# Attention and a gated MLP on one core: plain fp32 products with v in the first four head pairs, new planner durations, and a weight decode that works through PSUM

## The chip, the cores and the metric

The kernel runs on one core of a Trainium2 chip. Its time is the device time of one execution in microseconds (us). The profile shows five engines of the core: PE (TensorE: matrix products and transposes), DVE (VectorE), ACT (ScalarE), POOL (GpSimd) and SP (SyncE, which here only issues DMAs). Each engine runs its own list of instructions strictly in order and waits on semaphores for the others.

## What is computed

Attention with rotary embedding over 8 batches of 8 heads (sequence 576, head dimension 64), and then, on each batch, a gated MLP whose gate is mixed along the sequence.

```python
q_rot, k_rot = (rotate(q), rotate(k))
scores = scale * np.matmul(q_rot, k_rot.transpose(0, 1, 3, 2))
scores = scores - np.max(scores, axis=-1, keepdims=True)
attn = np.exp(scores)
attn = attn / (np.sum(attn, axis=-1, keepdims=True) + 1e-09)
return np.matmul(attn, v).astype(np.float32)
...
h = np.maximum(x @ w_in, 0.0)
u, v = (h[..., :d_ff // 2], h[..., d_ff // 2:])
...
v_n = (v - mu) / np.sqrt(var + 1e-06)
v_s = np.einsum('ts,bsd->btd', w_spatial, v_n) + b_spatial[None, :, None]
gated = u * v_s
return (gated @ w_out).astype(np.float32)
```

The inputs are float32, but the weights w_in and w_out come as 64-bit floats, so the kernel has to turn two 32-bit words into one float32 itself.

## The kernel before

**Precision.** Most products run on fp32r, a reduced float32 format of PE. To keep float32 accuracy an operand is split: ACT rounds it (`round_hi`, L298), a second engine subtracts the rounded part from the original (`rest_lo`, L301), and a product is made of three fp32r products: high by high, high by low, low by high.

**Attention.** The 64 heads are taken as 32 pairs, four to a batch. For each pair `prepare` loads q and k into two buffers `st` (stage), applies the rotation (L384 multiplies by a table half, L388 adds the two halves), splits them, copies rows into the stationary layouts `qs`, `ks`, `qz` by DMA, makes the low part of k (`lk`), and splits v into `vs` (ACT L298, POOL L423). `scores` makes nine score tiles of 128 x 576 for a pair (L459); DVE takes the row maximum (`nmx`, L467) and ACT the exponential with its row sum (`e`, L469). `values` works in three chunks of three tiles: PE turns the exponentials around 128 keys at a time (`tp`, L487), ACT takes the high part out of PSUM (`eh`, L498), DVE the low part (`el`, L301), and PE multiplies with v into `pv` (L511). In the first five pairs (`SUMMED = 5`) the three products of a step go one after the other into the same 64 rows of `pv`, and ACT copies them out (L525); in the later pairs high and low part of v are one operand 128 wide, ACT copies half of `pv` to `avt` (L535) and DVE adds the halves (L533). `normalise` sends the row sums through DRAM to spread them over partitions (`rt`, `rb`), multiplies (L565) and splits the result `x` for the MLP.

**MLP.** Four pairs make a batch; its MLP has four products: `pa` (W_in's second half, L599), `pb` (W_in's first half, L622), `pc` (along the sequence, L640) and `pd` (W_out, L655), with the normalisation on DVE and ACT between them.

**Weight decode.** `decode` handles 12 pieces of 128 x 512. Its five DVE steps (L328 twice, L334, L336, L337) shift, mask and combine the words, ACT does two (L333, and the high part), and the low part goes to POOL or DVE. All operands lie in SBUF. The steps of DVE are marked as holding the port that DVE and POOL share (`port=True`).

**Order.** Nothing is issued in the order written. Each step is entered in `Program` with a key, a duration per engine and the buffers it needs; `run` simulates the engines and, whenever one is free, issues the ready step with the lowest key, so the durations in the table and the numbers of buffers (`SLOTS`) decide what order the engines' lists have. A step with two costs (`pair_op`) goes to whichever engine takes it first. PSUM has two buffers for scores (`sc`), one for `pv` and three called `pm` for transposes and MLP products.

Of the kernel before, what the change touches and what calls it, by code (L numbers as in the profile page):

```python
# [211 lines left out]
def tile_attention_gated_mlp(  # L212
# [93 lines left out]
    def decode(key, where, at, src):  # L306
# [19 lines left out]

        def bits(out, w, s1, s2, op0, op1=None):
            return lambda: ts(out=out(), in0=word(w), scalar1=s1, scalar2=s2, op0=op0, **({"op1": op1} if op1 else {}))  # L328
# [5 lines left out]
        op(DVE, 600, key, lambda: stt(out=sg.tile, in0=word(1), scalar=-(2**31), in1=sg.tile, op0=ALU.bitwise_and, op1=ALU.bitwise_or), r=[t1], w=[sg], port=True)  # L334
        op(DVE, 335, key, bits(lambda: word(1), 1, 0xFFFFF, 0x100000, ALU.bitwise_and, ALU.bitwise_or), w=[t1], port=True)
        op(DVE, 602, key, lambda: stt(out=word(1, F32), in0=word(0, U32), scalar=2.0**-32, in1=word(1), op0=ALU.mult, op1=ALU.add), r=[t0], w=[t1], port=True)  # L336
        scaled = lambda: stt(out=sg.tile.bitcast(F32), in0=word(1, F32), scalar=2.0**-20, in1=sg.tile.bitcast(F32), op0=ALU.mult, op1=ALU.mult)  # L337
# [106 lines left out]
    def scores(i, a, t, lk, sm, key, e, n_e):
# [24 lines left out]
        op(ACT, 717, key + K_EXP, lambda: nc.scalar.activation(e[:, e0:e0 + S].rearrange("p (c n) -> p c n", c=2), tops(), AF.Exp, bias=nmx.tile, scale=1.0, accum_out=sm[:, at:at + 1]), r=[pt, nmx, *([(e, 0)] if n_e == 1 else [])], w=[(e, n_e), ("sums", i % 2, at)], new=[] if n_e == 1 else [e])  # L469
# [322 lines left out]
```

## Time and profile before

| | |
|---|---|
| time, median of 3 runs | 1005.13 us (1003.97 to 1006.08) |
| the profiled execution: its own time | 1004.86 us |
| the profiled execution: span of the trace | 1003.1 us |
| busy PE / DVE / ACT / POOL | 944.0 / 698.1 / 757.2 / 596.0 us |
| PE's granted clock, mean | 0.995 |
| DMA packets, bytes, mean rate | 56694, 126.19 MB, 126 GB/s |

The span runs from the first to the last instruction; the execution's own time is 1.8 us longer. A line of the profile names the kernel's line, the engine, the operation, and output <- input by the program's names; a row of the timeline starts with the start and the duration in us, and ends with the idle time ahead of it and what ended it. PE rows are pipelined: a product's duration includes its way through the array, so the distance between the starts of two rows is what a product costs in a stream.

### The profile page before, as it was taken

The page shows a single profiled execution, that of the slowest core. Times are in us where ns is not written, and L with a number is a line of the kernel's source. Part 1 is how long each engine was busy: PE and PEld are TensorE (multiplying, and loading weights), DVE is VectorE, ACT ScalarE, POOL GpSimd, SP SyncE. Part 2 cuts the span into 40 slices and gives each one's busy share as a digit, 9 for nine tenths or more (in the row PEclk, how much of TensorE's full clock was granted, in tenths as well). Part 3 has the DMA queues.
Part 4 walks back from the last instruction along what each step waited for, and adds up shares of the span by engine and source line. Part 5 has one row for each costly group of instructions (what it writes and reads, how often), then busy time and mean ns, then how long its engine had stood idle before and what let it go on. Part 6 is the DMA issues. An engine that isn't in the chain of part 4 may idle for free.

```text
span 1003.1 us, 19763 instructions
## 1 busy us (share of the span) xinstructions
PE 944.0 (94%) x6692; PEld 874.5 (87%) x6692; DVE 698.1 (70%) x1557; ACT 757.2 (75%) x1850; POOL 596.0 (59%) x512
## 2 busy tenths in 40 slices
PE   3868888999999999999999999999999999999998
PEld 2657767999889998999989998899989998899898
DVE  6888989886776758676676767766576766767340
ACT  4877788777887778777787778877797777977452
POOL 3665666566566757566576756657675765773121
PEclk9999999999999999999999999999999999999999
DMA  8786443445453454445533464443544355431101
GB/s 276 219 226 198 134 135 77 119 106 157 130 134 94 116 152 122 122 116 158 147 88 104 122 170 125 126 128 88 153 119 131 104 159 145 104 88 32 60 1 48
DMA packets 56694, 126.19 MB, mean 126 GB/s; under 512 B 13329, under 2 KB 13329, under 8 KB 56594
## 3 DMA queue, kind: packets, MB, share of 16 engines
q1 hardware_dynamic: 56594, 124.94, 45.6%
q8 instruction: 53, 0.87, 0.4%
q14 instruction: 47, 0.39, 0.1%
HBM read 66.03 MB, written 9.58 MB: 75 GB/s over the span
## 4 chain that ended last, share of the span: by engine, by line
PE 57%; ACT 18%; DVE 11%; DMA 8%; issue 4%; SPq 2%; POOL 0%; ACTq 0%; DVEq 0%; POOLq 0%
PE pc L640 10%; PE tp L487 9%; PE sc L459 9%; PE pd L655 9%; PE pv L511 9%; PE pb L622 7%; ACT e L469 5%; ACT eh L498 5%; PE pa L599 4%; DMA st<-in_qk_dram 3%; DVE nmx L467 2%; SPq L295 2%; DMA qs<-st 2%; DVE el L301 2%; ACT vv L682 2%
## 5 line engine op out<-in xcount | busy, mean ns | idle before, releaser
L498 ACT ACTIVATE eh<-tp 128x384 fp32r<-128x384 f32 (+1 forms) x576 | 246.7, 432 | 73.7 <-PE tp L487 69.7
L301 DVE TENSOR_TENSOR el<-tp,eh 128x384 fp32r<-128x384 f32 x384 | 210.6, 551 | 87.4 <-ACT eh L498 83.7
L469 ACT ACTIVATE e<-sc,nmx 128x576 f32<-128x576 f32 x288 | 213.4, 741 | 46.7 <-DVE nmx L467 43.3
L467 DVE TENSOR_REDUCE nmx<-sc 128x1 f32<-128x576 f32 x288 | 215.4, 750 | 44.0 <-PE sc L459 41.5
L487 PE MATMUL tp<-ident,e 128*128 128x128 f32 x1344 | 227.3, 276 | 16.1 <-DVE el L301 9.5
L487 PEld LDWEIGHTS tp<-ident,e 128*128 128x128 f32 x1344 | 165.9, 139 | 39.1 <-issue 10.8
L511 PE MATMUL pv<-eh,vs 128*128 128x384 f32 (+3 forms) x740 | 193.6, 319 | 2.6 <-ACT x L525 1.9
L384 POOL TENSOR_TENSOR st<-st,tabq 128x576 f32<-128x576 f32 x57 | 82.0, 1449 | 147.6 <-DMA st<-in_qk_dram 136.7
L459 PE MATMUL sc<-ks,qs 128*128 128x288 f32 x640 | 139.1, 308 | 24.4 <-DMA ks<-st 16.9
L622 PE MATMUL pb<-x,wi 128*128 128x288 f32 x768 | 144.1, 308 | 7.8 <-DVE eh L301 4.5
L640 PE MATMUL pc<-wsp,vn 128*128 128x288 f32 x768 | 143.8, 304 | 1.7 <-DVE eh L301 1.7
L655 PE MATMUL pd<-g,wo 128*128 128x288 f32 x768 | 142.3, 304 | 1.0 <-DVE el L301 0.4
L459 PEld LDWEIGHTS sc<-ks,qs 128*128 128x128 f32 x640 | 105.6, 193 | 35.0 <-issue 16.4
L511 PE MATMUL pv<-el,vs 128*64 128x192 f32 (+1 forms) x512 | 130.6, 296 | 2.0 <-DVE el L301 2.0
L599 PE MATMUL pa<-wi,x 128*128 128x512 f32 x448 | 131.0, 405 | 0.0
L622 PEld LDWEIGHTS pb<-x,wi 128*128 128x128 f32 x768 | 113.7, 190 | 14.6 <-PE pb L622 5.3
L459 PE MATMUL sc<-lk,qz 128*128 128x288 f32 x576 | 124.8, 299 | 0.0
L511 PEld LDWEIGHTS pv<-eh,vs 128*128 128x128 f32 (+1 forms) x740 | 116.5, 175 | 9.3 <-ACT x L525 2.9
L640 PEld LDWEIGHTS pc<-wsp,vn 128*128 128x128 f32 x768 | 114.7, 189 | 5.1 <-PE sc L459 2.9
L655 PEld LDWEIGHTS pd<-g,wo 128*128 128x128 f32 x768 | 113.8, 189 | 5.1 <-ACT ob L658 1.6
L301 DVE TENSOR_TENSOR eh<-tp,eh 64x256 fp32r<-64x256 f32 x192 | 68.3, 356 | 70.9 <-ACT eh L498 59.6
L459 PEld LDWEIGHTS sc<-lk,qz 128*128 128x128 f32 x576 | 93.9, 191 | 0.0
(139 smaller groups left out, 1372.8 us busy)
## 6 DMA issues: line engine op xcount, KB each, us to landing
st<-in_qk_dram SPq DMA_DIRECT2D x64, 576.0 KB
ks<-st SPq DMA_DIRECT2D x128, 160.0 KB
qs<-st SPq DMA_DIRECT2D x128, 144.0 KB
vr<-in_v_dram SPq DMA_DIRECT2D x32, 320.0 KB
qz<-st SPq DMA_DIRECT2D x64, 144.0 KB
out_dram<-ob SPq DMA_DIRECT2D x32, 288.0 KB
ws<-in_w_spT_dram SPq DMA_DIRECT2D x2, 576.0 KB
tabs<-in_tab_dram SPq DMA_DIRECT2D x1, 576.0 KB
```

The source lines that it names most:

```text
L301: eng.tensor_tensor(out=lo, in0=src, in1=hi.bitcast(F32), op=ALU.subtract)
L384: f = lambda e: e.tensor_tensor(out=st[j][:, cols], in0=st[j][:, cols], in1=(tabs if j else tabq)[:, cols], op=ALU.mult)
L459: nc.tensor.matmul(pt[:, c * 512:c * 512 + HALF], lhsT=lhsT, rhs=rhs[:, k0 + c * HALF:k0 + (c + 1) * HALF], start=(n == 0), stop=(n == len ...
L467: op(DVE, 665, key + K_MAX, lambda: nc.vector.tensor_reduce(out=nmx.tile, in_=tops(), op=ALU.max, axis=AX.XY, negate=True), r=[pt], w=[nmx ...
L469: op(ACT, 717, key + K_EXP, lambda: nc.scalar.activation(e[:, e0:e0 + S].rearrange("p (c n) -> p c n", c=2), tops(), AF.Exp, bias=nmx.tile ...
L487: nc.tensor.transpose(out=tp[:e.shape[1], m * P:m * P + P], in_=e, identity=ident)
L498: nc.scalar.activation(h, p, AF.Copy)
L511: nc.tensor.matmul(pv[0:rows, c1:c2], lhsT=vs[:, kt, h, vp, :], rhs=part[:, c1:c2], start=(kt == 0 and n == 0 and c1 == 0), stop=last)
L599: nc.tensor.matmul(pm.tile, lhsT=lhsT, rhs=win[1, d][:, j, :], start=(d == 0 and n == 0), stop=(d == 3 and n == len(todo) - 1))
L622: nc.tensor.matmul(pm[:, :HALF], lhsT=win[0, d][:, i, f * P:(f + 1) * P], rhs=x[d][:, at:at + HALF], start=(d == 0 and n == 0), stop=(d == ...
L640: nc.tensor.matmul(pm[:, :HALF], lhsT=lhsT, rhs=rhs, start=(t == 0 and n == 0), stop=(t == 4 and n == 1))
L655: nc.tensor.matmul(pm[:, :HALF], lhsT=wout[d,][:, i, m * P:(m + 1) * P], rhs=gs[d][:, at:at + HALF], start=(d == 0 and n == 0), stop=(d == ...
```

## The change

Three things change together.

The first four pairs (`PLAIN = 4`) get a routine of their own, `attention_plain`. They are no longer split: `e` is turned around as before, but each transposed block is copied out of PSUM once (`et`, by ACT or DVE, whichever the planner finds free) and multiplied as plain fp32 with the v that was loaded (`vr`). The two heads of a pair go to rows 0 to 63 and 64 to 127 of `pv`. The tiles are grouped differently: a first chunk of six tiles (three of each head) and a second of three, where tile 4, which holds the tails of both heads, needs a small copy on POOL (`e1`). The splitting of v and the adds are gone there. All later pairs, pair 4 now included, use the 128-wide form.

The decode keeps its intermediate in one of the three `pm` buffers of PSUM instead of SBUF, so that each DVE step has at most one operand in SBUF and no longer claims the shared port; the low part always goes to DVE.

The table is changed: durations of many small steps, POOL's cost, the decode's keys, and `SLOTS` (among others `vs` from 2 to 1, `vraw` from 1 to 2, `e2` from 3 to 5, `e1` from 4 to 2, `eh` from 8 to 7). In `normalise` the add of 1e-9 to the row sums moves from DVE to ACT.

```diff
 SLOTS = {
-    "stage": 2, "lk": 1, "vraw": 1, "vs": 2, "e2": 3, "e1": 4, "eh": 8, "rb": 1, "x32": 1, "avt": 1, "xg": 7, "m": 4,
-    "small": 4, "nmx": 3, "rt": 2, "sc": 2, "pv": 1, "pm": 3,
+    "stage": 2, "lk": 1, "vraw": 2, "vs": 1, "e2": 5, "e1": 2, "eh": 7, "rb": 1, "x32": 1, "avt": 1, "xg": 7, "m": 4,
+    "small": 3, "nmx": 3, "rt": 2, "sc": 2, "pv": 1, "pm": 3,
...
-DEC_V = [4, 22, 22, 56]
+DEC_V = [30, 40, 50, 60]
...
-    return 148 + n * 21 // 10
+    return 150 + n * 32 // 15
...
+        pt = Buf("pm", None, None, f"dc{n}")
...
-        op(DVE, 335, key, bits(lambda: sg.tile, 1, 20, 0x7FF, ALU.logical_shift_right, ALU.bitwise_and), r=[t1], w=[sg], new=[sg], port=True)
...
-        op(DVE, 602, key, lambda: stt(out=word(1, F32), in0=word(0, U32), scalar=2.0**-32, in1=word(1), op0=ALU.mult, op1=ALU.add), r=[t0], w=[t1], port=True)
...
-        pair_op(HF, key, lambda e: rest_lo(e, where[at][:, 1, :], sg.tile.bitcast(F32), where[at][:, 0, :]), r=[sg, (n, "hi")], w=[n])
+        op(DVE, 640, key, bits(20, 0x7FF, ALU.logical_shift_right, ALU.bitwise_and), r=[t1], w=[pt], new=[pt])
...
+        op(DVE, 640, key, lambda: stt(out=pt.tile, in0=word(0, U32), scalar=2.0**-32, in1=ints(), op0=ALU.mult, op1=ALU.add), r=[t0], w=[pt])
...
+        op(DVE, 640, key, lambda: rest_lo(nc.vector, where[at][:, 1, :], pt.tile, where[at][:, 0, :]), r=[pt, (n, "hi")], w=[n])
...
+        if i < PLAIN:
+            return
         op(ACT, 627, key + K_V, lambda: round_hi(vs[:, :, :, 0, :], vr.tile), r=[vr], w=[(vs, 0)], new=[vs])
...
+    def values_plain(i, c, pieces, pairs_e, e1, vr, x32, key):
...
+            op(PE, 110 * n, at, transpose, r=["ident", *whole_e, *([] if name.endswith("_0a") else held)], w=[tp], new=[tp])
+
+            def evacuate(e):
+                if e == ACT:
+                    nc.scalar.activation(et[:, :n * P], tp[:, :n * P], AF.Copy)
+                else:
+                    nc.vector.tensor_copy(out=et[:, :n * P], in_=tp[:, :n * P])
+
+            last = [chain[-1]] if name.endswith(f"_{NQ - 1}") else []
+            prog.either({ACT: act_ns(n * P), DVE: dve_ns(n * P)}, at + K_HI, evacuate, r=[tp, *held], w=[et, *last], new=[et], port=False)
+            return et
...
+                    out = pv[64 * h:64 * h + 64, :n]
...
+                        nc.tensor.matmul(dst, lhsT=vr[r0:r1, kt, h, :], rhs=rhs, start=(kt == 0 and m == 0), stop=(kt == 4 and m == len(cols) - 1))
+
+            op(PE, nq * 21 // 11 + 90, at + K_AV, multiply, r=[vr, *dict.fromkeys(p[0] for p in parts)], w=[pv], new=[pv] if kt == 0 else [])
...
-        op(DVE, 75, key + K_INV, lambda: nc.vector.tensor_scalar(out=sm[:, 0:9], in0=sm[:, 0:9], scalar1=1e-9, scalar2=None, op0=ALU.add), w=need)
+        op(ACT, 100, key + K_INV, lambda: nc.scalar.activation(sm[:, 0:9], sm[:, 0:9], AF.Copy, bias=1e-9), w=need)
...
-        attention(i)
+        (attention_plain if i < PLAIN else attention)(i)
```

Since the table decides the order, the lists of all engines change. Three places follow. In a name the first number is the head pair (`st2_0`: pair 2, q) and the last one tells buffers apart.

**DVE, in pair 0's products with v.** Before:

```order
L301 TENSOR_TENSOR el0_0_0_225<-tp0_0_0_198,eh0_0_0_212 128x384
L467 TENSOR_REDUCE nmx0_0_4_234<-sc0_0_4_204 128x1
L301 TENSOR_TENSOR el0_0_1_244<-tp0_0_1_214,eh0_0_1_228 128x384
L301 TENSOR_TENSOR el0_0_2_252<-tp0_0_2_230,eh0_0_2_242 128x384
L467 TENSOR_REDUCE nmx0_1_0_259<-sc0_1_0_218 128x1
L301 TENSOR_TENSOR el0_0_3_269<-tp0_0_3_246,eh0_0_3_257 128x384
L467 TENSOR_REDUCE nmx0_1_1_279<-sc0_1_1_261 128x1
L328 TENSOR_SCALAR sgwi12_290<-wi12raw_196 128x512
L301 TENSOR_TENSOR eh0_0_4_281<-tp0_0_4_273,eh0_0_4_281 64x2x128
L301 TENSOR_TENSOR eh0_0_4_281<-tp0_0_4_273,eh0_0_4_281 64x128
```

and now:

```order
L587 COPY et0_0_0a_240<-tp0_0_0a_222 128x384
L587 COPY et0_0_0b_251<-tp0_0_0b_228 128x384
L341 TENSOR_SCALAR dcwi11_257<-wi11raw_197 128x512
L500 TENSOR_REDUCE nmx0_0_4_268<-sc0_0_4_244 128x1
L341 TENSOR_SCALAR dcwi12_274<-wi12raw_226 128x512
L347 SCALAR_TENSOR_TENSOR sgwi11_286<-wi11raw_197,dcwi11_257 128x512
L341 TENSOR_SCALAR dcwi11_257<-wi11raw_197 128x512
L648 RECIPROCAL sums0_68<-sums0_68 128x9
L349 SCALAR_TENSOR_TENSOR dcwi11_257<-wi11raw_197,dcwi11_257 128x512
L649 STREAM_TRANSPOSE rt0_307<-sums0_68 128x32
L587 COPY et0_0_2b_309<-tp0_0_2b_295 128x384
L350 SCALAR_TENSOR_TENSOR dcwi11_257<-dcwi11_257,sgwi11_286 128x512
```

The low parts `el` and `eh` of the exponentials are replaced by copies `et` (some of them; the others are ACT's), and the decode of wi11 and wi12, which stood at other places, now stands between them. In the whole list all twelve pieces are decoded ahead of the first product `pb` of the MLP; before, eight were.

**POOL, preparing pair 2** (`st2`, `lk2`), with what belongs to pair 0's result (`x32_0`, `x0`). Before, from the first rotation on:

```order
L384 TENSOR_TENSOR st2_0_435<-st2_0_435,tabq_65 128x576 x2
L423 TENSOR_TENSOR vs2_549<-vr2_223,vs2_549 128x10x64
L301 TENSOR_TENSOR st2_0_435<-st2_0_435 128x576
L565 TENSOR_TENSOR x32_0_339<-x32_0_339,rb0_545 128x576
L301 TENSOR_TENSOR wi12_623<-sgwi12_290,wi12_623 128x512
L301 TENSOR_TENSOR x0_635<-x32_0_339,x0_635 128x576
L301 TENSOR_TENSOR x0_635<-x32_0_339,x0_635 128x64
L384 TENSOR_TENSOR st2_1_503<-st2_1_503,tabs_64 128x576
L388 TENSOR_TENSOR st2_1_503<-st2_1_503 128x576
L301 TENSOR_TENSOR wt2_72<-wst_617,wt1_71 64x576
L301 TENSOR_TENSOR lk2_768<-st2_1_503 128x576
L301 TENSOR_TENSOR lk2_768<-st2_1_503 128x64
```

and now:

```order
L396 TENSOR_TENSOR st2_0_347<-st2_0_347,tabq_65 128x576 x2
L400 TENSOR_TENSOR st2_0_347<-st2_0_347 128x576
L396 TENSOR_TENSOR st2_1_411<-st2_1_411,tabs_64 128x576
L309 TENSOR_TENSOR st2_0_347<-st2_0_347 128x576
L396 TENSOR_TENSOR st2_1_411<-st2_1_411,tabs_64 128x576
L653 TENSOR_TENSOR x32_0_396<-x32_0_396,rb0_452 128x576
L400 TENSOR_TENSOR st2_1_411<-st2_1_411 128x576
L309 TENSOR_TENSOR x0_536<-x32_0_396,x0_536 128x576
L309 TENSOR_TENSOR x0_536<-x32_0_396,x0_536 128x64
L309 TENSOR_TENSOR lk2_575<-st2_1_411 128x576
L309 TENSOR_TENSOR lk2_575<-st2_1_411 128x64
```

Pair 2's two halves of the rotation stand together: the split of v (`vs2`) and the decode's low part (`wi12`) are gone from between them, and pair 0's `x0` has moved behind the last rotation sum of `st2_1`.

**PE, from pair 8's last product with v to pair 9's first.** Before:

```order
L511 MATMUL pv8_2_3695<-eh8_2_4_3738,vs8_2978 128x384
L459 MATMUL sc9_1_1_3791<-ks1_79,qs1_77 128x288 x2
L459 MATMUL sc9_1_1_3791<-lk9_3491,qz_80 128x288 x2
L622 MATMUL pb1_00_3781<-x5_2539,wi01_1525 128x288 x3
L487 MATMUL tp9_0_2_3807<-ident_66,e2_9_0_3584 128x128 x2
L487 MATMUL tp9_0_2_3807<-ident_66,e1_9_0_3660 128x128
L622 MATMUL pb1_00_3781<-x6_3000,wi02_2103 128x288 x3
L511 MATMUL pv9_0_3820<-eh9_0_0_3760,vs9_3399 128x384
```

and now:

```order
L543 MATMUL pv8_2_3386<-eh8_2_4_3428,vs8_3082 128x384
L492 MATMUL sc9_1_1_3476<-ks1_79,qs1_77 128x288 x2
L492 MATMUL sc9_1_1_3476<-lk9_3141,qz_80 128x288 x2
L710 MATMUL pb1_00_3468<-x5_2287,wi01_702 128x288 x3
L519 MATMUL tp9_0_2_3491<-ident_66,e2_9_0_3215 128x128 x2
L519 MATMUL tp9_0_2_3491<-ident_66,e1_9_0_3347 128x128
L710 MATMUL pb1_00_3468<-x6_2703,wi02_1002 128x288 x3
L519 MATMUL tp9_0_3_3506<-ident_66,e2_9_0_3215 128x128 x2
L519 MATMUL tp9_0_3_3506<-ident_66,e1_9_0_3347 128x128
L710 MATMUL pb1_00_3468<-x7_3133,wi03_918 128x288 x3
L543 MATMUL pv9_0_3526<-eh9_0_0_3443,vs9_3484 128x384
```

Between the two products stand now nine products of `pb` and six transposes, where it was six and three: `vs9` can be written only when `pv8` has read `vs8`. On ACT the writing of `vs9` stands directly ahead of the copy of pair 8's half of `pv`:

```order
L306 ACTIVATE vn_73<-vv1_2_3325 128x512
L530 ACTIVATE eh9_0_1_3474<-tp9_0_1_3455 128x384
L306 ACTIVATE vs9_3484<-vr9_2672 128x10x64
L560 ACTIVATE avt8_2_3495<-pv8_2_3386 64x384
L765 ACTIVATE sm1_3_3426<-sm1_3_3426 128x1
L306 ACTIVATE st10_1_3255<-st10_1_3255 128x576
```

Before, with two buffers, `vs9` was written while pair 8 was being multiplied.

More of the change, by code (lines that the diff above doesn't have):

```diff
@@ L334, in decode @@
[L334 to L337, printed above, removed]
@@ L441, in attention, with attention_plain @@
             values(i, c, spans, e2, e1, vs, x32, key, None if n == 0 else todo[0][1])
+        normalise(i, sm, x32, 20 * i)
+    def attention_plain(i):
+        lk, vr = prepped[i]
+        sm = sums[i % 2]
+        x32 = Buf("x32", [P, S], F32, f"x32_{i}")
+        for c, (tiles, pieces) in enumerate(CHUNKS2):
+            pairs_e = []
+            e1 = None
+            for n, (a, t) in enumerate(tiles):
+                if t == 4:
+                    e1 = e = Buf("e1", [P, S + TW], F32, f"e1_{i}")
+                elif a == 0:
+                    e = Buf("e2", [P, 2 * S], F32, f"e2_{i}_{t}")
+                    pairs_e.append(e)
+                scores(i, a, t, lk, sm, 20 * i + S_AT2[c][n], e, a)
+                if t == 4:
+                    op(POOL, pool_ns(TW), 20 * i + S_AT2[c][n] + K_EXP, lambda: nc.gpsimd.tensor_copy(out=e1[:, S:], in_=e1[:, 4 * P:S]), r=[(e1, 0)], w=[(e1, 1)])
+            values_plain(i, c, pieces, pairs_e, e1, vr, x32, 20 * i + VALUES_AT2[c])
         normalise(i, sm, x32, 20 * i)
@@ L511, in multiply @@
                         nc.tensor.matmul(pv[0:rows, c1:c2], lhsT=vs[:, kt, h, vp, :], rhs=part[:, c1:c2], start=(kt == 0 and n == 0 and c1 == 0), stop=last)
-            passes = [64, 64] if summed else [P]
-            ns = sum(pe_ns(c2 - c1, m) for _, c1, c2, _ in spans for m in (passes + [64] if lo else passes))
-            op(PE, 110 * (3 if lo else 2), at, transpose, r=["ident", (e2, 0), (e2, 1), (e1, 2)], w=[tp], new=[tp])
-            op(ACT, act_ns(CW) + 51 * (not lo), at + K_HI, high, r=[tp, *held], w=[(hi, 0), *([n] if kt == 4 else [])], new=[hi])
-            op(DVE, dve_ns(CW) + 68 * (not lo), at + K_LO, low, r=[tp, (hi, 0)], w=[lo or (hi, 1)], new=[lo] if lo else [])
+            passes = [P, 64] if lo else [P]
+            ns = sum(pe_ns(c2 - c1, m) for _, c1, c2, _ in spans for m in passes)
+            op(PE, 110 * (3 if lo else 2), at, transpose, r=["ident", (e2, 0), (e2, 1), (e1, 2), *(held if kt else [])], w=[tp], new=[tp])
+            op(ACT, act_ns(CW) if lo else 672, at + K_HI, high, r=[tp, *held], w=[(hi, 0), *([n] if kt == 4 else [])], new=[hi])
+            op(DVE, dve_ns(CW) if lo else 755, at + K_LO, low, r=[tp, (hi, 0)], w=[lo or (hi, 1)], new=[lo] if lo else [])
             op(PE, ns, at + K_AV, multiply, r=[(vs, 0), (vs, 1), (hi, 0), lo or (hi, 1)], w=[pv], new=[pv] if kt == 0 else [])
@@ L521, in values @@
         new = [x32] if before is None else []
-        if summed:
-            def copy():
-                for rows, to, cols in pieces:
-                    nc.scalar.activation(x32[rows, to], pv[0:64, cols], AF.Copy)
-            op(ACT, act_ns(CW) + 51 * (len(pieces) - 1), key + K_HALF, copy, r=[pv, *first], w=[(x32, c)], new=new)
-            return
         tmp = Buf("avt", [64, CW], F32, f"avt{n}")
@@ L533, in add @@
                 nc.vector.tensor_tensor(out=x32[rows, to], in0=pv[0:64, cols], in1=tmp[:, cols], op=ALU.add)
-        op(ACT, act_ns(CW), key + K_HALF, lambda: nc.scalar.activation(tmp.tile, pv[64:P, :CW], AF.Copy), r=[pv], w=[tmp], new=[tmp])
-        op(DVE, dve_ns(CW) + 68 * (len(pieces) - 1), key + K_ADD, add, r=[pv, tmp, *first], w=[(x32, c)], new=new)
+        op(ACT, 440, key + K_HALF, lambda: nc.scalar.activation(tmp.tile, pv[64:P, :CW], AF.Copy), r=[pv], w=[tmp], new=[tmp])
+        op(DVE, dve_ns(CW) + 170 * (len(pieces) - 1), key + K_ADD, add, r=[pv, tmp, *first], w=[(x32, c)], new=new)
```

89 lines of the change are left out of this document (68 added, 21 removed).

## The prediction

> **What bounds the kernel now.** PE's busy tenths in 40 slices of 25 us come first:
>
> ```profile
> PE   3868888999999999999999999999999999999998
> ```
>
> PE is full from the eighth slice on and has gaps before. The second view is the busy time by stage, cut at the first score, at the fifth pair's first score and at the first `pb`:
>
> ```profile
> core 0: us, PE busy (x) PEld busy (x) DVE busy (x) ACT busy (x) POOL busy (x), PEclk, DMA share, GB/s
> 15.60:115.60 100.00, 81.09 (x538) 67.73 (x538) 89.11 (x157) 79.44 (x196) 60.33 (x46) 0.97 0.72 207
> 115.60:155.80 40.20, 35.96 (x224) 29.29 (x225) 35.28 (x77) 31.66 (x79) 27.38 (x20) 1.00 0.43 125
> 155.80:200.00 44.20, 38.78 (x273) 35.95 (x271) 40.17 (x79) 36.34 (x86) 25.23 (x20) 0.96 0.41 107
> 200.00:980.00 780.00, 768.53 (x5517) 722.12 (x5516) 522.71 (x1229) 598.76 (x1471) 474.12 (x404) 1.00 0.43 116
> ```
>
> From 200 us on PE is busy 768.5 of 780 us: there only PE's own work, or a new wait of PE, moves the time. In the start it is otherwise. From 15.6 to 155.8 us (140.2 us) DVE is busy 124.4 us (89%), PE 117.1 (83%), ACT 111.1 (79%), POOL 87.7 (63%). DVE is the fullest, and PE's idle time there, 23 us, and another 5.4 us up to 200, is what a better start can win. Third view, the cuts themselves, from the timeline and from the rows of `pb`:
>
> ```profile
> 15.60 0.82 PE L459 MATMUL sc<-ks,qs 128*128 128x288 f32 x2 [15.60 <-DMA ks<-st]
> 66.32 0.50 PE L459 MATMUL sc<-ks,qs 128*128 128x288 f32 x2 [2.72 <-DMA rt1d<-rt]
> 115.57 0.51 PE L459 MATMUL sc<-ks,qs 128*128 128x288 f32 x2 [0.41 <-DMA ks<-st]
> L622 PEld LDWEIGHTS pb<-x,wi x768: 186/188/332, 155.8 to 971.4; 128*128 128x128 f32 x192
> ```
>
> Pairs 0, 2 and 4 begin at 15.6, 66.3 and 115.6: 25 us a pair. Each begins with a wait for a DMA, the last step of its preparation. Since PE works through nearly the same list afterwards, what the first `pb` gains at 155.8 us is carried to the end. I reckon against the profiled execution, 1004.86 us with a span of 1003.1; it lies 0.03% under the median of the three runs, and about 0.2% is what a measurement of this kernel can tell from no change.
>
> **DVE in the start.** The groups of 15.6 to 155.8 us, DVE's, and ACT's copy up to 115.6:
>
> ```profile
> L301 DVE TENSOR_TENSOR el<-tp,eh 128x384 fp32r<-128x384 f32 x61 | 32.6, 549 | 6.3 <-ACT eh L498 5.8
> L301 DVE TENSOR_TENSOR eh<-tp,eh 64x256 fp32r<-64x256 f32 x15 | 6.3, 418 | 1.9 <-ACT eh L498 1.4
> L301 DVE TENSOR_TENSOR eh<-tp,eh 64x128 fp32r<-64x128 f32 x15 | 4.4, 293 | 0.2
> L384 DVE TENSOR_TENSOR st<-st,tabq 128x576 f32<-128x576 f32 x5 | 5.8, 1180 | 0.1
> L559 DVE TENSOR_SCALAR sums<-sums 128x9 f32<-128x9 f32 x5 | 2.4, 490 | 0.2 <-ACT e L469 0.2
> L498 ACT ACTIVATE eh<-tp 128x384 fp32r<-128x384 f32 x48 | 22.4, 487 | 5.2 <-PE tp L487 5.0
> ```
>
> A pair loses 12 low parts of 549 ns and three pairs of small ones, 12 x 0.549 + 3 x (0.418 + 0.293) = 8.7 us of DVE; four pairs 34.9 us. It gains plain copies: the order gives DVE 21 of the 56, between ACT's 487 ns and the two-operand 549 each; at 0.52 that is 10.9 us. Five rotation halves fewer (5 x 1.18) save 5.9, the moved add to the sums 2.4; the fifth pair's adds and small shifts cost some 1 us.
>
> The decode goes the other way. The stretch of its four DVE lines (L336, L328, L334, L337) up to the first `pb`, busy us and steps, and three single rows:
>
> ```profile
> 15.60:155.80 140.20, 7.08 (x8) 0.98 0.64 183
> 15.60:155.80 140.20, 7.76 (x14) 0.98 0.64 183
> 15.60:155.80 140.20, 4.06 (x6) 0.98 0.64 183
> 15.60:155.80 140.20, 6.24 (x8) 0.98 0.64 183
> L328 DVE TENSOR_SCALAR wi11raw<-wi11raw x1: 425/425/425, 15.5 to 15.5; 128x512 int32<-128x512 int32 x1
> L336 DVE SCALAR_TENSOR_TENSOR wi11raw<-wi11raw x1: 683/683/683, 18.6 to 18.6; 128x512 f32<-128x512 uint32 x1
> L336 DVE SCALAR_TENSOR_TENSOR wi13raw<-wi13raw x1: 1909/1909/1909, 69.6 to 69.6; 128x512 f32<-128x512 uint32 x1
> ```
>
> So 36 of the 60 steps, 25.1 us, fall into the start now; some 4 lie ahead of it and 20 behind, at the same 0.70 us each 14 us. The order puts all twelve pieces, with six DVE steps each, ahead of the first `pb`. A step through PSUM is in no row; it lies between the 425 ns of the one-operand step and the 683 ns of the two-operand step, and I take the upper one for all: 72 x 0.68 = 49 us, less some 1.5 before the first score, which is 22 us more in the start (at 425 ns it would be 4 more). What the last row has beyond 683 ns, 1.2 us at a time when POOL was busy, should go. The Trainium skill (SBUF — State Buffer, "SBUF: two separate sides") says that DVE with two SBUF inputs and a POOL instruction that reads SBUF exclude each other for a whole instruction; the 683 and 1909 agree, and by it the new steps run at their own length. The same skill (VectorE: DVE Perf Modes, "Why PSUM operands drop a tier") has float32 steps with a PSUM operand lose the doubled rate, which speaks against the 425 ns and leaves the sum as it is.
>
> Sum on DVE: -34.9 + 10.9 - 5.9 - 2.4 + 1 + 22 = -9 us (with short decode steps -27). ACT loses 4 x 15 rounded parts, takes 35 of the copies and also ends some 10 us lower, with slack already. At 89% occupancy DVE's -9 is -10 us of time.
>
> **The preparation of a pair.** A pair cannot begin before its preparation; for pair 2 the rows of SP and POOL are:
>
> ```profile
> 38.51 0.46 SPq L295 DMA_DIRECT2D st<-in_qk_dram  x1
> 42.60 2.81 POOL L384 TENSOR_TENSOR st<-st,tabq 128x576 f32<-128x576 f32 x2 [0.30 <-DMA rt0d<-rt]
> 47.68 1.56 POOL L423 TENSOR_TENSOR vs<-vr,vs 128x640 fp32r<-128x640 f32 x1 [2.27 <-ACT vs L298]
> 52.48 1.28 POOL L301 TENSOR_TENSOR wi<-sgwi,wi 128x512 fp32r<-128x512 f32 x1
> 55.36 1.42 POOL L384 TENSOR_TENSOR st<-st,tabs 128x576 f32<-128x576 f32 x1
> 60.05 2.55 SPq L295 DMA_DIRECT2D ks<-st  x4
> ```
>
> From the load at 38.5 to the first score at 66.3 pass 28 us, and between the rotation's halves POOL waits 2.27 us for ACT, splits v (1.56) and makes a decode's low part (1.28): 5.1 us that the new order takes out of the chain for each of the first pairs. Half a rotation more on POOL (1.4 us) stands against it. So DVE allows -10 us by the first `pb`, the chain up to -15 (four pairs at 3.7). I take -13: DVE's bound was made with the long end of the decode. Twelve loads of weights are moved too, past others on SP, at about the 0.46 us of issue of the first row each; the DMA share of 0.72 in the start leaves room for them.
>
> **From the first `pb` to 200 us.** The 14 us of decode leave DVE, which is 91% busy there, and PE lacks 5.4 us: I take -4, between 0 and -5.4.
>
> **PE's work with v.** Products in the present form, transposes and MLP products in a stream:
>
> ```profile
> 62.38 0.51 PE L511 MATMUL pv<-eh,vs 128*64 128x384 f32 x2
> 62.73 0.34 PE L511 MATMUL pv<-el,vs 128*64 128x384 f32 x1
> 62.91 0.51 PE L511 MATMUL pv<-eh,vs 128*64 128x384 f32 x2
> ...
> 304.16 0.64 PE L622 MATMUL pb<-x,wi 128*128 128x288 f32 x3
> 304.64 0.49 PE L487 MATMUL tp<-ident,e 128*128 128x128 f32 x3
> 304.88 0.42 PE L511 MATMUL pv<-eh,vs 128*128 128x384 f32 x1
> ```
>
> A product of 384 columns costs 0.175 us, a step of three 0.53, a pair 3 x (4 x 0.53 + 0.35) = 7.4 us. The new pair has ten plain products of 384 columns and ten of 192. No row has one. The only plain fp32 operands on PE are the transposes, three (384 columns) in 0.24 us, with the 0.08 that the row behind them is late 0.32; at that a pair costs 10 x 0.32 + 10 x 0.16 = 4.8 us. The ends are the fp32r rate (2.6 us) and four partial products of 0.175, as two split operands have them (10.5 us). For four pairs that is -10, between -19 and +12. I put it at 0: PE has 23 us of idle cover there. Pair 4 loses 5 x 0.175 x 3 = 2.6 us of PE where PE is 89% busy and pays 1.2 us of DVE adds: -1.
>
> **One buffer for the split v.** From pair 5 on `vs` has to wait for the pair before. The present boundary and the two writers:
>
> ```profile
> 338.06 0.42 PE L511 MATMUL pv<-eh,vs 128*128 128x384 f32 x1
> 340.06 0.44 PE L511 MATMUL pv<-eh,vs 128*128 128x384 f32 x1
> 341.53 0.73 ACT L298 ACTIVATE vs<-vr 128x640 fp32r<-128x640 f32 x1
> 342.46 1.56 POOL L423 TENSOR_TENSOR vs<-vr,vs 128x640 fp32r<-128x640 f32 x1
> ```
>
> From the start of the last product to the next pair's first the new chain needs 0.42, then ACT to POOL 0.93, then 1.56, and the 0.2 that lay between ACT's end and POOL once more to reach PE: 3.1 us. PE's own rows between, at 0.13 a product of 288 columns and 0.32 for three transposes, come to 2.6 us from pair 8 to 9, 3.1 from 9 to 10, 4.1 from 10 to 11 and 2.9 from 11 to 12, and so on in every batch. So PE lacks 0.5 + 0 + 0 + 0.2 us in four boundaries, 27 of them about 5 us. Behind the waiting ACT step stand the copy of `avt`, for which DVE's add and the only `pv` buffer wait, and behind POOL's the multiplication of `x32`. Other changed durations in the table only reorder, worth about -1. I take +4.
>
> **Sum.** -13 - 4 + 0 - 1 + 4 = -14: 1004.9 - 14 = 991 us.
>
> **Rivals.** (1) The start shrinks further: the copies can go to either engine, short decode steps save up to 18 us of DVE, POOL's waits go. With the chain at its -15, another -5 where decode steps no longer block POOL, -5 up to 200 us and no wait for `vs`: 979 us. For it speaks that DVE's rows held the port against POOL for 1.2 us at a time; against it, that two decodes hold two of the three `pm` buffers in the order shown.
> (2) Plain products are slow: each streams its columns four times and the heads do not overlap, 0.70 us for 384 columns. PE then has 117 + 12 = 129 us of work up to the first `pb` and cannot go under 136 at 95%: -4 there, -4, -1, +4 give 1000 us. The Trainium skill (FP8 and Floating Point Precision, "TensorE Precision Notes") states four passes for true fp32; no row here shows it, and the two heads' separate rows of `pv` may overlap.
> (3) Slower: the single `vs` buffer. If ACT reaches its step one exponential late (0.74 us) at each boundary, PE waits 0.9 us, 27 x 0.9 = 25 us, and 1005 - 18 + 25 = 1012. It outweighs the start from 18 / 27 = 0.67 us a boundary on. ACT is 77% busy from 200 us on, which speaks for some lateness; against it, the step stands where the planner expects it free.
> (4) No change: the pairs still begin with DMAs, whose queue now carries the weight loads between them, and the 25 us a pair stay: 1004 us.
>
> **Chances.** The forecast 0.55 (984 to 998), (1) 0.17, (2) 0.10, (3) 0.12, (4) 0.06. Faster by over 0.2%, below 1003: the forecast, (1) and most of (2), 0.80; within 0.2%: 0.07; slower: 0.13. The range runs from 972, the case (1) with the cheap ends of the products with v, to 1008.
>
> **What would show it.** The first `pb` near 143 us instead of 155.8, pair 4's first score before 107; DVE still about 89% busy in the start; decode steps of 0.6 to 0.7 us with none over 1 us; no `el` rows before pair 4; plain products of about 0.3 us per 384 columns; PE waiting at most 0.5 us for `vs` rows of POOL. It would be wrong if the first `pb` stands where it did, or if PE's idle time from 200 us on grows from 11 us to over 25.

## The result, and the profile after

Four runs of the changed kernel took 986.37 to 990.44 us, median 989.39; the kernel before has 1005.13. The ratio is 0.984, 95% interval 0.982 to 0.986. The profiled execution took 989.69 us with a span of 987.9. The forecast was 991 us in a range of 972 to 1008. In one run below, e8_vs1_small, the profiled execution went at a clock of 0.855; it is left out of that run's median and ratio, and nothing is read from its trace.

PE's busy tenths, each slice now 24.7 us:

```profile
PE   2888999999999999999999999999999999999998
```

PE is full from the fifth slice on, where it was from the eighth. The busy time by stage, cut as before at the first score, pair 4's first score, the first `pb` and 44.2 us later:

```profile
core 0: us, PE busy (x) PEld busy (x) DVE busy (x) ACT busy (x) POOL busy (x), PEclk, DMA share, GB/s
15.50:103.00 87.50, 74.84 (x441) 49.82 (x441) 78.56 (x131) 69.67 (x165) 59.72 (x51) 0.98 0.79 233
103.00:141.60 38.60, 38.28 (x243) 30.57 (x244) 33.91 (x76) 31.24 (x79) 19.24 (x14) 1.00 0.48 138
141.60:185.80 44.20, 43.87 (x332) 42.31 (x331) 34.94 (x76) 36.97 (x93) 21.38 (x19) 1.00 0.49 121
185.80:965.80 780.00, 764.40 (x5464) 714.93 (x5463) 521.62 (x1185) 596.29 (x1482) 471.69 (x403) 1.00 0.43 115
```

Up to the first `pb` there are 126.1 us instead of 140.2. DVE is busy 112.5 of them, 89% as before, with 11.9 us less to do; PE is busy 113.1 of them (74.84 + 38.28), 90% where it was 83%, so that now both are equally full. In the next 44.2 us PE lacks 0.3 us instead of 5.4; in the 780 us after that it lacks 15.6 instead of 11.5. From the first `pb` to the end there are 987.9 - 141.6 = 846.3 us, before 847.3: **the whole gain is made in the start**, and behind it one thing was won and another lost. The rows of pairs 2, 3 and 4 and of `pb`, from the timeline and the list of instructions:

```profile
58.66 0.54 PE L492 MATMUL sc<-ks,qs 128*128 128x288 f32 x2
81.60 0.53 PE L492 MATMUL sc<-ks,qs 128*128 128x288 f32 x2
102.97 0.50 PE L492 MATMUL sc<-ks,qs 128*128 128x288 f32 x2 [0.95 <-DMA ks<-st]
L710 PE MATMUL pb<-x,wi x768: 288/295/407, 141.7 to 956.2; 128*128 128x288 f32 x192
```

A pair takes (102.97 - 15.48) / 4 = 21.9 us instead of 25.0. Where pair 2 waited 2.72 us for a DMA, it now follows at once; of pairs 1 to 4 only pair 4 still waits for one, 0.95 us.

DVE's groups in the stretch up to the first `pb`: the copies' line, then the four lines of decode steps (L341 twice a piece, L347, L349, L350), then the decode's low parts:

```profile
15.50:141.60 126.10, 11.38 (x21) 0.99 0.69 204
15.50:141.60 126.10, 14.85 (x22) 0.99 0.69 204
15.50:141.60 126.10, 7.47 (x11) 0.99 0.69 204
15.50:141.60 126.10, 7.57 (x11) 0.99 0.69 204
15.50:141.60 126.10, 7.57 (x11) 0.99 0.69 204
...
L309 DVE TENSOR_TENSOR wi<-dcwi,wi 128x512 fp32r<-128x512 f32 x8 | 5.5, 684 | 0.4 <-ACT wi L306 0.4
L309 DVE TENSOR_TENSOR wo<-dcwo,wo 128x512 fp32r<-128x512 f32 x4 | 2.7, 674 | 0.1
L350 DVE SCALAR_TENSOR_TENSOR dcwi<-dcwi,sgwi x8: 685/688/699, 14.8 to 85.2; 128x512 f32<-128x512 f32 x8
```

The 21 copies cost 11.4 us (10.9 were reckoned). The decode costs 14.85 + 7.47 + 2 x 7.57 + 5.5 + 2.7 = 45.7 us (49 - 1.5 = 47.5 reckoned), and no step is over 0.70 us. A plain product looks like this on PE:

```profile
30.52 0.54 PE L616 MATMUL pv<-et_0a,vr 128*64 128x384 f32 x1
30.52 0.54 PE L616 MATMUL pv<-et_0b,vr 128*64 128x384 f32 x1
30.89 0.49 PE L616 MATMUL pv<-et_0a,vr 128*64 128x384 f32 x1
30.90 0.49 PE L616 MATMUL pv<-et_0b,vr 128*64 128x384 f32 x1
```

Each product is two instructions, 0.37 us from start to start, and the two heads, which fill different 64 columns, start together. So each product lasts some 0.7 us, but two of them share that time: about 0.35 us a product, where 0.32 was taken.

### The profile page after: what moved, and what is told of

It is laid out like the page before. It is cut to its first block, busy times and chain, and to the rows that moved or that the text cites. A ratio compares the mean times of both kernels' runs of the same rounds, so it can differ in the third digit from the quotient of the medians.

```text
span 987.9 us, 19563 instructions
## 1 busy us (share of the span) xinstructions
PE 940.0 (95%) x6612; PEld 855.9 (87%) x6612; DVE 679.7 (69%) x1483; ACT 743.5 (75%) x1835; POOL 580.0 (59%) x508
## 4 chain that ended last, share of the span: by engine, by line
PE 60%; ACT 16%; DMA 8%; DVE 7%; POOL 4%; issue 3%; SPq 1%; ACTq 0%; POOLq 0%; DVEq 0%
PE pc L728 12%; PE sc L492 11%; PE pv L543 9%; PE tp L519 9%; PE pd L743 6%; PE pb L710 6%; PE pa L687 5%; DMA st<-in_qk_dram 4%; ACT e L502 3%; ACT eh L530 3%; ACT vv L770 2%; POOL st L396 2%; DVE nmx L500 2%; POOL st L400 2%; DMA qs<-st 2%
## 5 line engine op out<-in xcount | busy, mean ns | idle before, releaser
L530 ACT ACTIVATE eh<-tp 128x384 fp32r<-128x384 f32 (+1 forms) x504 | 216.8, 433 | 86.9 <-PE tp L519 81.1
L309 DVE TENSOR_TENSOR el<-tp,eh 128x384 fp32r<-128x384 f32 x336 | 185.8, 554 | 72.3 <-ACT eh L530 63.2
L519 PE MATMUL tp<-ident,e 128*128 128x128 f32 (+1 forms) x1176 | 196.9, 273 | 8.8 <-DVE eh L309 5.2
L396 POOL TENSOR_TENSOR st<-st,tabq 128x576 f32<-128x576 f32 x60 | 84.6, 1428 | 174.6 <-DMA st<-in_qk_dram 152.7
L519 PEld LDWEIGHTS tp<-ident,e 128*128 128x128 f32 (+1 forms) x1176 | 145.2, 138 | 27.0 <-PE pd L743 5.6
L492 PE MATMUL sc<-ks,qs 128*128 128x288 f32 x640 | 142.1, 312 | 22.8 <-DMA ks<-st 16.4
L543 PE MATMUL pv<-eh,vs 128*128 128x384 f32 (+1 forms) x560 | 157.9, 323 | 4.2 <-DVE sm L766 2.0
L543 PE MATMUL pv<-el,vs 128*64 128x384 f32 (+1 forms) x448 | 113.5, 294 | 0.0
L543 PEld LDWEIGHTS pv<-eh,vs 128*128 128x128 f32 x560 | 97.1, 188 | 14.3 <-POOL vs L437 6.6
L309 DVE TENSOR_TENSOR eh<-tp,eh 64x256 fp32r<-64x256 f32 (+1 forms) x168 | 59.8, 356 | 67.4 <-ACT eh L530 41.6
```

Source lines behind the costliest of these rows:

```text
L309: eng.tensor_tensor(out=lo, in0=src, in1=hi.bitcast(F32), op=ALU.subtract)
L396: f = lambda e: e.tensor_tensor(out=st[j][:, cols], in0=st[j][:, cols], in1=(tabs if j else tabq)[:, cols], op=ALU.mult)
L492: nc.tensor.matmul(pt[:, c * 512:c * 512 + HALF], lhsT=lhsT, rhs=rhs[:, k0 + c * HALF:k0 + (c + 1) * HALF], start=(n == 0), stop=(n == len ...
L519: nc.tensor.transpose(out=tp[:e.shape[1], m * P:m * P + P], in_=e, identity=ident)
L530: nc.scalar.activation(h, p, AF.Copy)
L543: nc.tensor.matmul(pv[0:rows, c1:c2], lhsT=vs[:, kt, h, vp, :], rhs=part[:, c1:c2], start=(kt == 0 and n == 0 and c1 == 0), stop=last)
```

## The experiments

The first seven runs undo one part of the change, do one part of it alone, or touch one number. The question: is the gain a sum of parts, as the prediction reckoned (plain products freeing VectorE, decode, and a table of durations that "only reorders"), or does one part carry it? The columns: median time, ratio to before with its interval, first `pb`, time from the first to the last `pb`, and what PE lost to a lower clock in the first 300 us (over slices of 10 us, 10 x (1 - granted clock), from the stages of each trace).

| run | us | ratio | first pb | first to last pb | clock loss |
|---|---|---|---|---|---|
| before | 1005.13 | | 156.0 | 815.5 | 5.1 |
| the change | 989.39 | 0.984 (0.982 to 0.986) | 141.7 | 814.5 | 1.7 |
| e1_split_v | 1012.49 | 1.007 (1.005 to 1.009) | 166.8 | 818.0 | 3.4 |
| e2_sbuf_decode | 1008.83 | 1.003 (1.002 to 1.005) | 154.9 | 822.3 | 15.3 |
| e3_old_durations | 1016.65 | 1.013 (1.010 to 1.016) | 147.6 | 834.8 | 1.7 |
| e4_before_durations | 1000.79 | 0.994 (0.992 to 0.996) | 151.6 | 810.4 | 3.4 |
| e5_before_decode | 1013.50 | 1.008 (1.005 to 1.011) | 170.0 | 810.2 | 13.6 |
| e6_before_plain | 1018.00 | 1.012 (1.009 to 1.014) | 146.2 | 839.5 | 8.5 |
| e7_exp_735 | 994.54 | 0.989 (0.986 to 0.992) | 152.4 | 809.9 | 6.8 |
| e8_vs1_small | 983.24 | 0.978 (0.976 to 0.980) | | | |
| e9_vs2_small | 988.84 | 0.985 (0.983 to 0.987) | 143.6 | 816.9 | 3.4 |
| e10_old_dur_vs2 | 1016.58 | 1.012 (1.010 to 1.014) | 152.7 | 833.3 | 5.1 |
| e11_plain_twice | 1000.31 | 0.995 (0.994 to 0.997) | 156.0 | 811.8 | 0.0 |
| e12_max_twice | 1009.40 | 1.005 (1.003 to 1.006) | 163.6 | 811.2 | 10.2 |

The last three columns come from the profiled execution alone, whose own time can lie off the median: 1018.22 us in e1, 995.41 in e4 (the fastest of its eight), 994.12 in e9, 1019.43 in e10. Where the order differs, the place of the first `pb` within PE's list differs too, so that column and the next are read together.

**e1_split_v** (the function `values` is that of before, with its own four durations):

```diff
-PLAIN = 4
+PLAIN = 0
+SUMMED = 5
...
```

> The change without its plain products: the first four pairs multiply with the split v again, in the three-step 64-column form of before, pair 4 too; decode through PSUM, durations, buffers and due times as changed. Theory (the start is bound by VectorE, and the plain form takes 34.9 - 10.9 = 24 us of it away): the first pb moves from 141.6 us back to 155 to 165, and the time is 1003 to 1013 us. Rival A (the planner's numbers and due times bring the gain): 988 to 993. Rival B (the decode brings it): 988 to 993 too; the next two runs tell A from B.

1012.49 us, as the theory had it at its upper end. The time is 23 us over the change, about the 24 us of VectorE. But it is also 7 us over *before*, although it keeps the new decode, most of the durations and the due times: these help nothing without the plain products. It also keeps the changed numbers of buffers, and no run tells what those cost it.

**e2_sbuf_decode** (the function `decode` is that of before):

```diff
-        op(DVE, 640, key, bits(20, 0x7FF, ALU.logical_shift_right, ALU.bitwise_and), r=[t1], w=[pt], new=[pt])
+        op(DVE, 335, key, bits(lambda: sg.tile, 1, 20, 0x7FF, ALU.logical_shift_right, ALU.bitwise_and), r=[t1], w=[sg], new=[sg], port=True)
...
```

> The change with the decode of before (steps with both operands in SBUF, low part on either engine), at the changed due times; all else as changed. Theory (72 new steps of 0.69 us are 49.5 us of VectorE against 60 old ones of 0.70 us, 42 us, and the old ones only hold the port against GpSimd and give it the low parts of 1.28 us): 988 to 996 us, first pb at 141 to 147. Rival B (the decode brings the gain): 1000 to 1005 us.

1008.83 us: the theory's 988 to 996 is missed by 13 us, and rival B's 1000 to 1005 by 4. A step that holds both operands in SBUF can last as long as POOL's work beside it. The timeline of DVE, POOL, ACT and PE at one place, 28 us behind the first `pb`:

```profile
183.30 1.91 DVE L342 SCALAR_TENSOR_TENSOR sgwo<-wo2raw,sgwo 128x512 int32<-128x512 int32 x1
...
182.78 1.88 POOL L396 TENSOR_TENSOR st<-st 128x576 f32<-128x576 f32 x1
...
187.72 1.23 ACT L306 ACTIVATE wo<-sgwo 128x512 fp32r<-128x512 f32 x2 [5.84 <-DVE sgwo L345]
...
183.59 0.95 PE L706 MATMUL pb<-x,wi 128*128 128x288 f32 x6
189.88 0.85 PE L488 MATMUL sc<-ks,qs 128*128 128x288 f32 x2 [5.34 <-ACT e L498]
```

Eight decode steps stand in a row on DVE from 182.34 to 188.22, POOL's step beside the second takes 1.88 us instead of 1.42, ACT waits 5.84 us and the scores 5.34 us. Of the row's 5.9 us only some 1.6 are such stretching (1.2 in the step shown); the rest is that the order puts eight steps together. The row after the gap takes 0.85 us where the first of pair 2 in the change took 0.54: PE's clock is lowered. This kernel loses 15.3 us to that clock, the change 1.7. So up to 13.6 of the 19 us between the two can be the clock; how the rest divides between stretched steps and the other order is open.

**e3_old_durations** (fifteen durations of before in the change; two of them):

```diff
-    return 150 + n * 32 // 15
+    return 148 + n * 21 // 10
...
-        op(ACT, 730, key + K_EXP, ...
+        op(ACT, 717, key + K_EXP, ...
```

> The change with the planner's durations of before (GpSimd, exponential, small parts, sums of halves and the small steps of the normalisation), while plain products, decode, buffers and due times stay as changed. Theory (the durations only reorder): 988 to 992 us. Rival A (they bring the gain): 998 to 1005 us.

1016.65 us, 27 us over the change: the rival's sign and more than its size. The same instructions in another order. Six us of it lie ahead of the first `pb`, 20 us behind it (834.8 instead of 814.5 from the first to the last). PE's two largest waits in this run from 200 to 960 us, and then the work of all engines in that stretch, first in this run and then in the change:

```profile
PE pv L543 <- POOL vs L437: 8.1, 7, 1.3
PE pa L687 <- DVE el L309: 4.3, 6, 0.7
```

```profile
200.00:960.00 760.00, 734.47 (x5214) 677.68 (x5214) 504.89 (x1135) 579.91 (x1436) 459.76 (x391) 1.00 0.43 117
```

```profile
200.00:960.00 760.00, 745.00 (x5319) 696.20 (x5318) 510.47 (x1161) 586.18 (x1457) 457.09 (x389) 1.00 0.43 116
```

In the same time PE does 105 matmul instructions fewer (5214 for 5319, the first numbers in brackets), and the first wait is that for the single `vs` buffer. So the next theory was that the recorded durations matter because they keep this wait short; the runs e4, e9 and e10 test it.

**e4_before_durations** (the reverse of e3: only durations, in the kernel before):

```diff
-    return 148 + n * 21 // 10
+    return 150 + n * 32 // 15
...
```

> The kernel before with nothing but the recorded durations in the planner (no plain products, decode in SBUF, two buffers for the split v, due times of before). Theory after the third run (the durations count only together with the single buffer for the split v, where they keep TensorE's wait short): 1000 to 1010 us, no wait for that buffer. Rival A (right durations make any order better): 980 to 996 us.

1000.79 us, 5 us under before (1005.92 beside it): inside the theory's range, but its rival's sign. No wait for the `vs` buffer is in the trace's list of PE's waits, as expected. The durations alone are a third of the change's gain, though 5 us is no more than e7 below shows for an arbitrary touch.

**e5_before_decode** (`decode` of the change in the kernel before):

```diff
-DEC_V = [4, 22, 22, 56]
+DEC_V = [30, 40, 50, 60]
...
```

> The kernel before with the decode through PSUM and the changed due times of its first four pieces alone. Theory (VectorE is the fullest engine of the start and the new steps cost it 7 us more): 1003 to 1015 us. Rival B (slow steps and the held port were what delayed the pairs): 990 to 999 us.

1013.50 us, 8 us slower than before (1005.92 beside it), as the theory said; the rival falls. VectorE's work up to the first `pb` grew by 8.8 us, but the loss to PE's clock grew too, by 8.5 us, so the price isn't VectorE's alone. Through PSUM the decode takes `pm` buffers, of which there are three and which the transposes need too. PE's timeline:

```profile
109.57 0.33 PE L515 MATMUL pv<-el,vs 128*64 128x384 f32 x1
115.08 0.90 PE L491 MATMUL tp<-ident,e 128*128 128x128 f32 x3 [5.17 <-DVE wo L301]
...
123.36 0.49 PE L491 MATMUL tp<-ident,e 128*128 128x128 f32 x3
```

The transposes wait 5.17 us for the low part of a piece of `w_out` to leave its `pm` buffer, and then run at half the clock (0.90 us for what takes 0.49 eight us later).

**e6_before_plain** (plain products with their order and buffers, but the durations, decode and due times of before):

```diff
-DEC_V = [30, 40, 50, 60]
+DEC_V = [4, 22, 22, 56]
...
-    return 150 + n * 32 // 15
+    return 148 + n * 21 // 10
...
```

> The change with the durations, the decode and its due times of before, so before plus plain products, their order and buffers. Theory (the start loses 24 us of VectorE and is some 10 us shorter by TensorE's idle time up to 200 us, but with the old durations TensorE waits for the single buffer of the split v, 20 us with its weight loads): 1000 to 1018 us, and the start no longer than in the third run. Rival C (the plain products alone bring the gain): 985 to 995 us.

1018.00 us, within the theory's range. The first `pb` stands at 146.2, 10 us earlier than before; from there to the last it takes 839.5 us instead of 815.5, so the start's gain is lost twice over behind it. From 200 to 960 us PE's products wait 8.6 us for `vs` and their weight loads 11.4, the 20 us of the theory; e10 below shows that taking such waits away does not bring the time back.

**e7_exp_735**:

```diff
-        op(ACT, 730, key + K_EXP, ...
+        op(ACT, 735, key + K_EXP, ...
```

> The change with a single number touched: the planner takes 735 ns instead of 730 for the exponential, no instruction differs, only their order. Theory (the recorded durations are right within a few per cent, so 5 ns of 730 change little): 987 to 993 us. Rival D (the order was picked among many, and any small change of a number costs several us): 994 to 1010 us.

994.54 us, 5 us over the change, just at the lower edge of rival D. Not one instruction differs. The clock loss grew by 6.8 - 1.7 = 5.1 us. So differences of about 5 us between two orders are within what one arbitrary touch of one number did, and only larger ones can be put down to a cause here.

**e8_vs1_small and e9_vs2_small**:

```diff
-    "stage": 2, "lk": 1, "vraw": 2, "vs": 1, "e2": 5, "e1": 2, "eh": 7, "rb": 1, ...
+    "stage": 2, "lk": 1, "vraw": 2, "vs": 1, "e2": 4, "e1": 2, "eh": 6, "rb": 1, ...   (e8)
+    "stage": 2, "lk": 1, "vraw": 2, "vs": 2, "e2": 4, "e1": 2, "eh": 6, "rb": 1, ...   (e9)
```

> Control for the next run: the change with e2 of four buffers instead of five and eh of six instead of seven, which makes room for a second buffer of the split v; that buffer is still single here. Theory: two buffers less cost a little, 988 to 1000 us. Rival D (order by luck): up to 1010.

> The same with two buffers for the split v. In the trace of the change TensorE's products wait for GpSimd's step of that buffer for 1.4 us and their weight loads for 6.6 us from 186 us on. Theory (that wait is on the path, 4 to 8 us): 3 to 8 us below the run before, and no row in which TensorE waits for that buffer. Rival (another wait takes its place): within 2 us of it.

e8 with 983.24 us beats both kernels, though it was meant as a control: fewer buffers gave another order. e9, with the second `vs` buffer, is 5.6 us slower than e8 and equal to the change. PE's largest wait and those for `vs` from 186 us on in the change, then PE's three largest in e9 from 200 us on:

```profile
PE tp L519 <- DVE eh L309: 5.2, 6, 0.9
...
PE pv L543 <- POOL vs L437: 1.4, 2, 0.9
...
PEld pv L543 <- POOL vs L437: 6.6, 12, 1.1
```

```profile
PE tp L519 <- ACT ob L746: 6.1, 5, 1.9
PE tp L519 <- ACT u L713: 3.2, 5, 0.8
PE pb L710 <- ACT u L713: 3.0, 7, 0.4
```

The wait for `vs` is gone, and transposes and products that wait for ACT to empty the MLP's buffers stand in its place. The theory of 4 to 8 us for the single buffer falls, as far as two orders can show that differ by so little.

**e10_old_dur_vs2** (e3's durations with e9's buffers):

> The change with the planner's durations of before (as in the third run, 1016.65 us) and the buffers of the run before this one, so two for the split v. In the third run products and weight loads waited 8.1 and 11.4 us for that buffer. Theory (the durations matter through that wait above all): 995 to 1004 us. Rival (the old durations cost as much elsewhere): 1010 to 1020 us.

1016.58 us, the same as e3's 1016.65. The theory formed after e3 falls too: with two `vs` buffers no wait for them is left, and the old durations still cost 27.7 us against e9. PE's two largest waits are others now:

```profile
PE tp L519 <- ACT ob L746: 9.5, 6, 2.0
PE pv L543 <- DVE x L558: 5.8, 10, 1.2
```

**e11_plain_twice and e12_max_twice.** The last two keep the planner's order and only lengthen one engine's work in the first four pairs. In e11 each plain product is issued twice, which doubles these pairs' result:

```diff
-                for et, h, r0, r1, c0, n in parts:
+                for rep, (et, h, r0, r1, c0, n) in enumerate(parts + parts):
...
```

> The change with each plain product issued twice into the same sum (the first four pairs' result is doubled). It adds some 0.72 us of TensorE for each step of two heads with 384 columns, about 5.4 us a pair, 21.6 us for four pairs, where TensorE is idle 13 us between 15.5 and 141.6 us. Theory (partly covered): 8 to 18 us slower than the change, 998 to 1008 us. Rival (the cover that the prediction used, 23 us, takes it all): 988 to 993 us. Rival (all on the path): 1010 us or more.

In e12 VectorE takes a maximum twice:

```diff
+            for _ in range(2 if i < PLAIN and t < 4 else 1):
+                nc.vector.tensor_reduce(out=nmx.tile, in_=tops(), op=ALU.max, axis=AX.XY, negate=True)
...
```

> The change with the maximum of 32 of the first four pairs' 36 score tiles taken twice by VectorE, in the planner's same order. Back to back a maximum takes 0.67 us, so VectorE gets 32 x 0.67 = 21.4 us more before the first pb, about what TensorE got in the run with the products twice, which cost 10.9 us. Theory (VectorE sets the length of the start): 18 to 22 us slower than the change, 1007 to 1012 us, more than twice the price of the same time on TensorE less what it hides. Rival (the preparation of the pairs through GpSimd and DMA sets it, VectorE has slack): 5 to 12 us slower, 994 to 1001 us.

e11 took 1000.31 us, 10.9 more than the change, e12 1009.40, 20.0 more. Both within the theory. The stage from the first score to the first `pb` in e11, then in e12, with the maxima of e12 and of the change in their own stages:

```profile
15.30:156.00 140.70, 129.81 (x851) 91.06 (x852) 114.31 (x207) 101.09 (x244) 78.58 (x65) 1.00 0.62 183
```

```profile
15.30:163.60 148.30, 122.15 (x684) 84.07 (x685) 135.66 (x240) 102.21 (x245) 78.70 (x65) 0.93 0.59 174
...
L502 DVE TENSOR_REDUCE nmx<-sc 128x1 f32<-128x576 f32 x82 | 60.4, 753 | 5.0 <-PE sc L492 3.9
```

```profile
L500 DVE TENSOR_REDUCE nmx<-sc 128x1 f32<-128x576 f32 x50 | 36.8, 753 | 8.8 <-PE sc L492 8.4
```

PE's work in the start grew by 129.8 - 113.1 = 16.7 us, and 10.9 us of it, two thirds, reached the end. VectorE got 32 maxima more, 21.4 us as reckoned and 23.2 by its busy time (135.7 for 112.5), and 20.0 us of it, about nine tenths, reached the end; at 135.7 of 148.3 us it is again busy 91%. Part of that price, up to 8.5 us, is PE's clock, which was lower beside VectorE's delays (10.2 us lost instead of 1.7), where e11 lost nothing to it. Without the clock the two prices could be nearly equal, some 11.5 and 12.6 us (20.0 - 8.5 and 10.9 + 1.7), by estimate.

## Why the prediction was right, point by point

**VectorE bounds the start: right in its terms, but not the whole account.** The start shrank by 14.1 us (13 forecast), with VectorE's share at 89% in both kernels and its work 11.9 us smaller (9 forecast). The terms hold: 21 copies, 11.4 us for 10.9; the decode, 45.7 us for 47.5. e12 agrees, since time added to VectorE comes out at the end almost whole, with the clock's part in it. But e11 and e12 are both made on the change, where PE is as full in the start as VectorE; they don't show that VectorE alone bound it before. And its work does not fix the length. The whole start, first score to first `pb`, of e3 and then of e7:

```profile
15.30:147.60 132.30, 114.83 (x684) 80.36 (x685) 112.52 (x207) 101.00 (x243) 77.88 (x65) 0.99 0.66 195
15.30:152.40 137.10, 119.92 (x693) 85.12 (x693) 112.01 (x206) 102.73 (x247) 82.04 (x69) 0.95 0.67 192
```

VectorE's work is that of the change, 112.5 and 112.0 us, but the starts are 6 and 11 us longer (e7's loses 5.1 us more to the clock and does 6.8 us more of PE's work there). So the order counts for six us or more of the start at the same VectorE work, and that 14.1 came so near to 13 is in part luck.

**The preparation of a pair: right in direction.** From pair 2's load to its first score it took 27.8 us. The load's row is now

```profile
36.76 0.46 SPq L303 DMA_DIRECT2D st<-in_qk_dram  x1
```

and the score follows at 58.66, 21.9 us later. The shorter chain is no bound: pairs 1 to 3 no longer wait for a DMA at all.

**From the first `pb` to 200 us: right.** -5.1 us, for -4. Up to 1.7 us of it is the clock, which the kernel before lost between 160 and 180 us and the change did not.

**Plain products counted at nothing: mis-sized.** The rate of 0.32 us was near (0.35). But "23 us of idle cover" is not cover: by e11 two thirds of what PE gets more in the start arrives at the end. By the same measure, going from 7.4 us a pair to some 5.3 us (five steps of 0.7 and five of half that) was worth some 4 x 2.1 x 2/3 = 5.6 us by estimate, which the sum had at zero. By e11's own 16.7 us, 4.2 a pair, it would be 8.5. Neither can simply be added to the 13 us of the start, which shrank by 14.1 in all; how much of that is PE's is not shown. The Trainium skill (FP8 and Floating Point Precision, "TensorE Precision Notes") gives true fp32 four passes; the trace agrees, with some 0.7 us a product against four times 0.175. Rival 2 took that price and let the heads run one after the other. They run side by side, so half of its price was wrong.

**One buffer for `vs`, +4: right in size by luck.** PE's idle time from 200 us on grew by 4.1 us. But of PE's own waits only 1.4 us bear that buffer's name, up to 0.9 us at a time where the prediction named 0.5 as the most; 6.6 us are waits of weight loads, which run beside PE's products. The largest of PE's waits, 5.2 us, is that of transposes for VectorE's `eh`. And e9 took the waits for `vs` away and gained nothing over the change, and lost 5.6 us against e8. What PE did not wait for there, it waited for at ACT. Rival 3 has no run on its side: e10 lost the same as e3 without any such wait.

**"Other changed durations in the table only reorder, worth about -1": the term that failed.** Put back, they cost 27 us (e3, and again in e10); alone in the kernel before they give 5 us (e4). The prediction counted edits one by one, and that was the fault in its form: from before, the three parts alone give -5 (durations), +8 (decode) and +12 us (plain products with their order and buffers), +15 in sum; together they give -16. The order is worked out from the durations, and the new lists and buffers suffer far more from the old ones than the kernel before did: from the first to the last `pb` e3 takes 20 us and e6 25 us more than the change, before only 5 us more than e4. What makes them so sensitive (fewer `e1` and `eh` buffers, say) is open; it is not `vs` alone.

**Left out: PE's clock.** The change lost 1.7 us to it in the first 300 us, before 5.1. That can be up to 3.4 us of the gain, and no term of the sum had it.

**Rival 1's reading of the slow decode step was the wrong way round.** It took the 1909 ns row, 69.65 us into the kernel before, as VectorE holding up POOL for 1.2 us. In that trace a step of POOL runs from 69.00 for 2.00 us instead of 1.40, so VectorE's step lost 1.2 us and POOL's 0.6.

So the total was right because the start and the stretch behind it came out near what was reckoned, and because the one term that was far off, the durations, does not show as long as the new order is made with the new table. Some of that is luck: orders of the same work differ by 5 us and more, and no term of the sum carried that.

## What to carry to other kernels

Repeating some of an engine's instructions in an unchanged order is a cheap way to see how far it sets the length of a stage: of 21 to 23 us added to VectorE 20.0 came out at the end, of 16.7 added to PE 10.9. Look at the clock too before reading such a price, and don't take the fullest engine as the only bound: the same VectorE work took 126 us in one order and 132 in another. Where a planner makes the order from a table of durations, an edit has no price of its own; price the edit with its table, and measure how far an arbitrary touch of one number moves the time (5 us in the one tried here) before putting a smaller difference down to a cause. A wait that bears a buffer's name isn't worth its length: look at who is late next.
